# Batches' rising rows turned round in DRAM ahead of their loads, in a fused Fourier and SwiGLU kernel

## The chip, the cores and the metric

The kernel runs on one core of a Trainium2 chip. The metric is device microseconds of one execution; the median of three runs is given. A profiled execution of the same program gives the rows that are quoted below. PE is TensorE, DVE is VectorE, ACT is ScalarE, POOL is GpSimd, SP is SyncE; an SPq row is an instruction with which SP's queue issues a transfer.

## The reference, cut to what matters

```python
def _attn_ref(x):                       # x: 8 batches, 3008 rows, 256 columns
    X = np.fft.fft(x, axis=1)
    X = np.fft.fft(X, axis=2)
    return X.real.astype(np.float32)

def _moe_ref(x, w_gate, w_val, w_out):  # x: 24064 x 256, d_ff 1536
    g = x @ w_gate
    silu = g * (1.0 / (1.0 + np.exp(-g)))
    val = x @ w_val
    return (silu * val @ w_out).astype(np.float32)
```

The output of the first function, its batches laid one after the other, is the input of the second.

## The kernel before, in words

The real part of the transform is even, so the kernel computes rows k and M − k of a batch from the same two halves, an even one (Pt) and an odd one (Qt): plus is their sum, minus their difference. The column transform is multiplied into the weights once (Wp from the cosines, Wq from the sines). The row transform is done per batch: POOL folds the batch's rows into sums and differences ("fold", lines 171 to 205), PE multiplies them with tables (line 1394), and DVE writes Pt and Qt.

**Tiles and units.** The 8 × 1504 columns of Pt and Qt are cut into 24 tiles of at most 512. A unit is one tile with one of twelve blocks of 128 of the 1536 hidden columns: gate and value by four or five matmuls of line 972, SiLU on ACT (1084, 1156, 1159), products for plus on DVE (1186) or POOL (1192), for minus on POOL (1183), which takes the pair buffer sv of two units. The output matmuls with Wo (1236) of one tile run beside the units of the next; ACT evicts them to ev (1243), and SP stores them (1249). A table KINDS gives each unit a digit: bit 0, the value's PSUM bank is filled ahead by ACT (line 1045) and copied out by ACT (1107), otherwise one DVE operation does both (1109); bit 1, the gate is split, with two gate matmuls and two DVE operations (1088, 1152) in place of three matmuls; higher bits, the value is copied by ACT (1189) and the product for plus, or both, go to POOL. The first fourteen units ("w") are done whole.

**Loads of a batch.** Each batch comes as two parts. XA holds 128 groups of rows, XC the other 60 (two batches share it, at partitions 0 and 64). The fold adds rising rows to falling rows, and the kernel wants both in falling order of the partition. "Down sets" are read in that order anyway: four transfers (line 142 for XA, 160 for XC). [...] Batch 0 is loaded once in rising order and turned by PE (line 435). For batch 1 the program writes the mixed order of up and down by hand (C1_ORDER, A1_ORDER); its XC is loaded at both halves of the partitions, by half down sets (line 164) and a copy within SBUF (169). Six of these go out ahead of the units.

**Order.** Behind the beginning, which is written out, a list of operations with engine, length, latency and place is put in order by a small planner (class Sched), which takes on each engine the operation that may start first within a window of places. Shifts (SHIFT) and a table by tile (BIAS_ROWS) move the places. The planner's loads count as SP operations with a time to issue, a landing and a ring time; SP is one queue in order, and each transfer waits for the eighth before it. Weight loads (line 391) and the load of Wo are issued by POOL.

**Steps that the prediction speaks of.** 13.92 us: two clears of XC's unused partitions from a tile of zeros (545). 18.9 us: first unit. 20.9 to 28: weight products for hidden columns 512 to 1535 (1442), whose operands land in XA's memory. 37.7: POOL copies tables (1546). 42.33: fold of batch 1's XC (178), 59.65: of its XA.

Of the kernel before, what the change touches and what calls it, by code (L numbers as in the profile page):

```python
# [12 lines left out]
F32 = mybir.dt.float32  # L13
# [6 lines left out]
def kernel(  # L20
# [8 lines left out]
    nc = tc.nc  # L29
    B, M, D = x.shape  # L30
    Dff = moe_w_gate.shape[1]
    P = 128
# [3 lines left out]
    R = M // 4  # L36
# [16 lines left out]
    NCR = GH - P  # L53
# [52 lines left out]
    XC = const.tile([P, 8, 2, D], F32, name="XC")  # L106
# [24 lines left out]

    JA, JC = P - LA + 1, GH - LC + 1

    C1_EARLY = 6
    C1_ORDER = "uuduuduuduuduumuueuueuece"
    A1_ORDER = "uuuuduuuuduuuuduuuud"

    def load_a(b, q):
        X3 = XA.rearrange("p a q d -> p a (q d)")
        res = ([lambda h=h: q.dma_start(out=X3[LA * h:LA * (h + 1), 0:4, :],  # L140
                                         in_=up_block(b, JA - LA * h, LA)) for h in range(NA)] +
                [lambda a=a: q.dma_start(out=X3[:, 4 + a, :], in_=down_set(b, a, JA, LA, NA)) for a in range(4)])
        return in_order(A1_ORDER, u=res[:NA], d=res[NA:]) if b == 1 else res

    def in_order(order, **todo):
        todo = {k: list(v) for k, v in todo.items()}
        return [todo[k].pop(0) for k in order]

    def load_c(b, q):

        X3 = XC.rearrange("p a q d -> p a (q d)")
        p0 = 64 * (b % 2)
        pm = p0 + NCR
        r = slice(p0, p0 + NCR)
        ups = [lambda h=h: q.dma_start(out=X3[p0 + LC * h:p0 + LC * (h + 1), 0:4, :],
                                       in_=up_block(b, JC - LC * h, LC)) for h in range(NC_)]
        mid = [lambda: q.dma_start(out=XC[pm:pm + 1, 0:4, 1],
                                   in_=rows_at(b, 0, [[R * D, 1], [R * D, 4], [1, D]]))]
        if b != 1:
            return ups + [lambda a=a: q.dma_start(out=X3[r, 4 + a, :], in_=down_set(b, a, JC, LC, NC_))  # L160
                          for a in range(4)] + mid

        def down(a, k):
            q.dma_start(out=XC[0:NCR, 4 + a, 0] if k else XC[r, 4 + a, 0],
                        in_=rows_at(b, R * (a + 1) - 2 * JC + k, [[2 * LC * D, NC_], [-2 * D, LC], [1, D]]))

        downs = [[lambda a=a, k=k: down(a, k) for a in range(4)] for k in range(2)]
        return in_order(C1_ORDER, u=ups, d=downs[0], e=downs[1], m=mid,
                        c=[lambda: q.dma_start(out=XC[0:NCR, 0:4, 1], in_=XC[r, 0:4, 0])])
# [82 lines left out]
    q = nc.sync  # L252
# [104 lines left out]
    sc = 2.0 * math.pi * (1.0 - 2e-7)  # L357
# [28 lines left out]
    def load_w(c, only):  # L386
        for i, src in ((0, moe_w_gate), (1, moe_w_val)):
            if i not in only:
# [13 lines left out]
                        in_=rows_at(0, 0, [[2 * R * D, 2], [R * D, 2], [1, D]]))  # L402
# [141 lines left out]
    for hi in range(2):  # L544
        q.dma_start(out=X3c[64 * hi + NCR:64 * hi + 64, :].rearrange("p (c d) -> p c d", d=D),
                    in_=zeros[64 * hi + NCR:64 * hi + 64].unsqueeze(1).to_broadcast([64 - NCR, 16, D]))
    loads_c1 = load_c(1, q)
    for load in loads_c1[:C1_EARLY]:
        load()
# [142 lines left out]
    A1_LOAD = 8  # L692
    ROW_1 = 12
    ROW_2 = 24
    ROW_3 = 35
    LOAD_AT = 2
# [45 lines left out]
    )  # L742
    BIAS = {(t, k): v for t, row in enumerate(BIAS_ROWS) for k, v in zip(SHIFT, row)}
# [11 lines left out]
    W_AT = (0.0, 2.0, 3.2, 4.6)  # L755
# [164 lines left out]
    def pool_us(n):  # L920
# [9 lines left out]
        "06ww20001013",  # L930
        "031303160011",
        "000010312133",
        "010210112012",
        "10110b103133",
        "001601031052",
        "300171700001",
        "331213005030",
        "010271031001",
        "34130b310300",
        "01b300700101",  # L940
        "21312101b300",
        "001371310011",
        "32120011b212",
        "10130b135030",
        "000135003170",
        "033170001011",
        "213b21011200",
        "103b10319610",
        "4030b13300b0",
        "616404563200",  # L950
        "143034169230",
        "706150233313",
# [21 lines left out]
    S = Sched()  # L974
# [310 lines left out]
    for b in range(2, B, 2):  # L1285
        u = slot[(b, 0)] - 1
# [6 lines left out]
    act_at = {}  # L1293
    spread_at = {}
    loads = []

    def run_loads(n):
        for what, k, fn in loads[:n]:
            up = k < (NA if what[0] == "A" else NC_)
            r, w, us, ring = [], [((what[0],), k)], 0.4 if up else 0.62, 0.57 if up or what[0] == "C" else 1.14  # L1300
            if what == ("A", 1):
                r = [(("C",), C1_ORDER.rindex("u"))]
                us, ring = (0.42, 0.75) if A1_ORDER[k] == "u" else (0.75, 1.1)
            if what == ("C", 1):
                us, ring = (0.48, 0.75) if C1_ORDER[k] == "u" else (0.95, 1.0)
                if C1_ORDER[k] == "c":
                    r = [(("C",), j) for j, o in enumerate(C1_ORDER) if o == "u"]
            S.add("SP", us, fn, r=r, w=w, after=[(("A",), "pre" if A1_ORDER[k] == "d" else "preW")] if what == ("A", 1) else [],
                  lat=2.5, ring=ring)
        del loads[:n]  # L1310
# [4 lines left out]
    def fold_step(what, i, unit):  # L1315
        kind, b = what
        q, j = (1, i) if what == ("C", 1) else divmod(i, 6)
        if i == 0:
            run_loads(max((k + 1 for k, (w_, _, _) in enumerate(loads) if w_ == what), default=0))
# [14 lines left out]
        r = {0: [((kind,), k) for k in range(40)], 1: [(tmp, "F")], 2: [(tmp, "F")], 3: [(tmp, "E"), (tmp, "O")],  # L1334
# [4 lines left out]
        if q == 1 and j == 0:  # L1339
            act_at.setdefault(max(unit + LOAD_AT, 15), []).append(what)  # L1340
# [6 lines left out]
    def load_next(what):  # L1347
        kind, b = what
        if kind == "A":
            if b + 1 < B:  # L1350
                loads.extend((("A", b + 1), k, fn) for k, fn in enumerate(load_a(b + 1, nc.sync)))
        else:
            b = b // 2 * 2 + 2
            if b < B:
                loads.extend((("C", b), k, fn) for k, fn in enumerate(load_c(b, nc.sync) + load_c(b + 1, nc.sync)))
# [248 lines left out]
    for k in range(C1_EARLY):  # L1604
        S.add("DMA", 0.01, lambda: None, w=[(("C",), k)], lat=2.0)
# [3 lines left out]
    S.add("DMA", 0.01, lambda: None, w=[(("pq", 0), "Q")], lat=0.1)  # L1609
# [7 lines left out]
    for i, u in enumerate(units):  # L1617
        t, f = u
# [3 lines left out]
        if i == 1:  # L1622
            loads.extend((("C", 1), k, fn) for k, fn in enumerate(loads_c1) if k >= C1_EARLY)
        if i == A1_LOAD:
            loads[0:0] = ((("A", 1), k, fn) for k, fn in enumerate(load_a(1, nc.sync)))
# [41 lines left out]
    S.run({'DVE': 1.6, 'ACT': 1.0, 'POOL': 1.4, 'PE': 0.0, 'SP': 2.0})  # L1667
# [30 lines left out]
```

## Time and profile before

| | |
|---|---|
| median of 3 runs | 599.71 us (597.59 to 600.29) |
| the profiled execution | 600.4 us |
| its span, first to last instruction | 598.6 us |
| mean granted TensorE clock | 0.999 |
| moved by DMA | 57.65 MB in 51082 packets |

The profiled execution's own time is 1.8 us longer than its span. Busy time counts an engine's instructions once where they overlap; a matmul's end is modelled, so a matmul of 512 columns is shown with 0.37 us though the next one starts 0.2 us after it. Waits are put down to the releaser that came last, and where it is a transfer its name can be that of another on the same semaphore.

### The profile page before, as it was taken

To read this page: it belongs to the slowest core of one execution; us is meant where nothing else is said; L and a number is where in the kernel's file an instruction comes from. 1 tells how busy PE (TensorE), PEld (TensorE's weight loads), DVE (VectorE), ACT (ScalarE), POOL (GpSimd) and SP (SyncE) were. 2 spreads that over 40 slices of the span, in tenths; PEclk is the share of its full clock that TensorE was granted. 3 is DMA by queue.
4 is the path that set the end of the run, shared out by engine and by line. 5 is a ranking of instruction groups with operands and counts; after the bars stand their busy time and mean duration, and the time that the engine had idled before them with its cause. 6 is when DMAs were issued, how large, how long until landed. Compare 5 with 4: busy or idle time off the path is not lost.

```text
span 598.6 us, 12468 instructions
## 1 busy us (share of the span) xinstructions
PE 587.0 (98%) x3953; PEld 389.2 (65%) x4012; DVE 570.3 (95%) x1064; ACT 557.4 (93%) x1080; POOL 527.8 (88%) x486
## 2 busy tenths in 40 slices
PE   7999999999999999999999999999999999999997
PEld 5456666666666666666666666666666666666686
DVE  8989999999999999999999999999999999999993
ACT  8778989989998999999999999999999999999995
POOL 8977999999899999998999998897986868687772
PEclk9999999999999999999999999999999999999999
DMA  9956347454715523454127122046221202111212
GB/s 247 150 110 115 109 121 141 132 140 117 178 46 107 136 70 113 123 129 138 57 55 166 46 62 82 19 115 161 63 64 37 65 19 80 48 46 53 60 54 81
DMA packets 51082, 57.65 MB, mean 96 GB/s; under 512 B 7283, under 2 KB 38439, under 8 KB 51017
## 3 DMA queue, kind: packets, MB, share of 16 engines
q1 hardware_dynamic: 47433, 53.91, 35.2%
q0 software_dynamic: 3216, 2.36, 2.8%
q8 instruction: 31, 0.51, 0.4%
q10 hardware_dynamic: 368, 0.59, 0.3%
q14 instruction: 34, 0.28, 0.2%
HBM read 29.43 MB, written 24.65 MB: 90 GB/s over the span
## 4 chain that ended last, share of the span: by engine, by line
PE 71%; ACT 8%; DMA 6%; DVE 4%; POOL 3%; issue 3%; SPq 1%; ACTq 0%; POOLq 0%; DVEq 0%
PE o L1236 30%; PE g L972 19%; PE v L972 16%; DMA XA<-in_x_dram 5%; ACT sv L1159 2%; PE o L1394 2%; PE g L1394 2%; ACT v L1045 2%; ACT es L1107 1%; POOL hm L1183 1%; DVE sv L1175 1%; ACT sp L1084 1%; DVE hp L1186 1%; ACT sp L1156 1%; ACT ev L1243 1%
## 5 line engine op out<-in xcount | busy, mean ns | idle before, releaser
L1183 POOL TENSOR_TENSOR hm<-sv 128x1024 bf16<-128x1024 f32 (+2 forms) x137 | 254.7, 1862 | 44.1 <-ACT sv L1159 17.7
L1175 DVE SCALAR_TENSOR_TENSOR sv<-es,v 128x512 f32<-128x512 f32 (+2 forms) x262 | 173.6, 668 | 5.4 <-PE v L972 2.8
L1236 PE MATMUL o<-Wo,hm 128*128 128x256 bf16 (+1 forms) x1128 | 163.6, 273 | 0.3
L1236 PE MATMUL o<-Wo,hp 128*128 128x256 bf16 (+1 forms) x1104 | 159.7, 273 | 0.2
L1186 DVE TENSOR_TENSOR hp<-sp,v 128x512 bf16<-128x512 f32 (+2 forms) x233 | 154.2, 668 | 2.8 <-PE v L972 2.0
L1236 PEld LDWEIGHTS <-hm 128*128 128x128 bf16 (+2 forms) x1140 | 111.8, 98 | 57.9 <-issue 2.5
L1236 PEld LDWEIGHTS <-hp 128*128 128x128 bf16 (+2 forms) x1140 | 111.9, 98 | 55.8 <-issue 0.9
L1159 ACT ACTIVATE sv<-g 128x512 f32<-128x512 f32 (+2 forms) x179 | 116.7, 671 | 4.6 <-PE g L972 2.3
L1084 ACT ACTIVATE sp<-g 128x512 f32<-128x512 f32 (+2 forms) x179 | 110.5, 621 | 4.1 <-PE g L972 2.7
L972 PE MATMUL v<-Pt,Wp 128*128 128x512 bf16 (+2 forms) x288 | 105.4, 375 | 1.8 <-DVE hp L1186 0.5
L972 PE MATMUL g<-Pt,Wp 128*128 128x512 bf16 (+2 forms) x280 | 104.4, 374 | 0.9 <-ACT sv L1159 0.7
L1045 ACT ACTIVATE v<-bc,w 128x512 f32<-128x512 bf16 (+2 forms) x146 | 104.6, 717 | 0.4
L1109 DVE SCALAR_TENSOR_TENSOR es<-bc,w,v 128x512 f32<-128x512 bf16 (+2 forms) x128 | 92.6, 731 | 2.4 <-ACT bc L1595 0.8
L1107 ACT ACTIVATE es<-v 128x512 f32<-128x512 f32 (+2 forms) x146 | 90.0, 618 | 3.8 <-PE g L972 1.0
L972 PE MATMUL g<-Qt,Wq 128*128 128x512 bf16 (+2 forms) x247 | 90.5, 374 | 0.4
L972 PEld LDWEIGHTS <-Wp 128*128 128x128 bf16 x576 | 56.3, 98 | 27.8 <-DVE Wp L505 0.7
L972 PE MATMUL g<-Qt,Wm 128*128 128x512 bf16 (+2 forms) x186 | 69.8, 375 | 0.2
L1088 DVE SCALAR_TENSOR_TENSOR sg<-bc,w,g 128x512 f32<-128x512 bf16 (+2 forms) x95 | 68.4, 723 | 1.4 <-PE g L972 0.7
L1159 ACT ACTIVATE sv<-sg 128x512 f32<-128x512 f32 (+2 forms) x95 | 65.1, 692 | 0.2 <-DVE sg L1152 0.2
L1152 DVE SCALAR_TENSOR_TENSOR sg<-sg,g 128x512 f32<-128x512 f32 (+2 forms) x95 | 62.9, 662 | 1.5 <-PE g L972 0.8
L1156 ACT ACTIVATE sp<-g 128x512 f32<-128x512 f32 (+2 forms) x95 | 57.7, 608 | 5.5 <-DVE sg L1152 5.3
L972 PE MATMUL v<-Qt,Wm 128*128 128x512 bf16 (+2 forms) x159 | 59.4, 374 | 0.8 <-ACT es L1107 0.4
(218 smaller groups left out, 759.1 us busy)
## 6 DMA issues: line engine op xcount, KB each, us to landing
out_dram<-ev SPq DMA_DIRECT2D x96, 128.0 KB
XA<-in_x_dram SPq DMA_DIRECT2D x30, 256.0 KB
XA<-in_x_dram SPq DMA_DIRECT2D x112, 64.0 KB
XC<-in_x_dram SPq DMA_DIRECT2D x28, 120.0 KB
XC<-in_x_dram SPq DMA_DIRECT2D x105, 32.0 KB
bc<-br SPq DMA_DIRECT2D x19, 128.0 KB
St<-Fc SPq DMA_DIRECT2D x12, 128.5 KB
out_dram<-ev SPq DMA_DIRECT2D x12, 120.0 KB
```

Of the source, the lines that this page charges most:

```text
L972: nc.tensor.matmul(ps[:, :n], Wt[:, gv, fs], src[:, :n], start=start, stop=stop, skip_group_check=True)
L1045: nc.scalar.activation(T_[kv][:, :w], bc[t][:, :w], AF.Copy, scale=w0[:, 1, f:f + 1])
L1084: nc.scalar.activation(sp_to()[:, :w], T_[kg][:, :w], AF.Silu)
L1088: nc.vector.scalar_tensor_tensor(T_[keg][:, :w], bc[t][:, :w], w0[:, 0, f:f + 1], T_[kg][:, :w], op0=Alu.mult, op1=Alu.add)
L1107: nc.scalar.activation(T_[kes][:, :w], T_[kv][:, :w], AF.Copy, scale=2.0 if on_pool(u) > 1 else 1.0)
L1109: nc.vector.scalar_tensor_tensor(T_[kes][:, :w], bc[t][:, :w], w0[:, 1, f:f + 1], T_[kv][:, :w], op0=Alu.mult, op1=Alu.add)
L1156: nc.scalar.activation(sp_to()[:, :wp], T_[kg][:, :wp], AF.Silu)
L1159: nc.scalar.activation(sv()[:, f % 2, w - 1::-1, 1], T_[kgm if by_dve else kg][:, :w], AF.Silu)
L1175: nc.vector.scalar_tensor_tensor(sv()[:, f % 2, w - 1::-1, 0], T_[kes][:, :w], 2.0, T_[kv][:, :w], op0=Alu.mult, op1=Alu.subtract)
L1183: nc.gpsimd.tensor_tensor(hts_(t)[1][:, f - 1:f + 1, :w], sv()[:, :, :w, 1], sv()[:, :, :w, 0], op=Alu.mult)
L1186: nc.vector.tensor_tensor(hts_(t)[0][:, f, :wp], T_[ksp][:, :wp], T_[kv][:, :wp], op=Alu.mult)
L1236: nc.tensor.matmul(st["ps"][:n, j, :], hts[t][minus][:, f, c:c + n], Wo[:, f, :], start=(f == 0), stop=(f == nF - 1))
```

## The change

Each later batch's rising rows are copied within DRAM to a scratch tile, in falling order of blocks (`reorder`, four copies per part: 256 KB each for XA, 120 KB for XC). XA's rising rows then come in two transfers, XC's in one, whose partitions step forward through the scratch tile. Down sets stay. For batch 1 the copies are issued in the written-out beginning; its XC is filled by eight half down sets and two loads of the turned copy, one for each half of the partitions. For batches 2 and 3 the copies are issued one with each unit from the eleventh on, later ones with every third unit; a load reads all copies that it needs. KINDS, BIAS_ROWS and some due times are new; their numbers are left out below, but for KINDS' counts: of 274 units that aren't whole, split gates go from 95 to 93, values filled ahead from 146 to 139, products for plus on POOL from 41 to 46, with 12 units that give POOL both as before.

```diff
-    C1_EARLY = 6
-    C1_ORDER = "uuduuduuduuduumuueuueuece"
-    A1_ORDER = "uuuuduuuuduuuuduuuud"
+    dram = ctx.enter_context(tc.tile_pool(name="turn", bufs=1, space=bass.MemoryType.DRAM))
+    scratch = {}
+
+    def reorder(kind, b, q):
+        n, L, N, j0 = (P, LA, NA, JA) if kind == "A" else (NCR, LC, NC_, JC)
+        t = scratch[kind, b] = dram.tile([4, N, 2 * L, D], F32, name=f"t{kind}{b}")
+
+        def one(a):
+            q.dma_start(out=t[a].rearrange("h r d -> r h d"),
+                        in_=rows_at(b, R * a + 2 * j0 - 1, [[D, 2 * L], [-2 * L * D, N], [1, D]]))
+
+        return [lambda a=a: one(a) for a in range(4)]
+
+    def reordered(kind, b, a0, a1):
+        return scratch[kind, b][a0:a1].rearrange("a h (i q) d -> (h i) a (q d)", q=2)
 
     def load_a(b, q):
         X3 = XA.rearrange("p a q d -> p a (q d)")
-        res = ([lambda h=h: q.dma_start(out=X3[LA * h:LA * (h + 1), 0:4, :],
-                                         in_=up_block(b, JA - LA * h, LA)) for h in range(NA)] +
+        return ([lambda a=a: q.dma_start(out=X3[:, a:a + 2, :], in_=reordered("A", b, a, a + 2)) for a in (0, 2)] +
                 [lambda a=a: q.dma_start(out=X3[:, 4 + a, :], in_=down_set(b, a, JA, LA, NA)) for a in range(4)])
-        return in_order(A1_ORDER, u=res[:NA], d=res[NA:]) if b == 1 else res
...
     def load_c(b, q):
-
         X3 = XC.rearrange("p a q d -> p a (q d)")
...
+        r = slice(64 * (b % 2), 64 * (b % 2) + NCR)
+        return ([lambda: q.dma_start(out=X3[r, 0:4, :], in_=reordered("C", b, 0, 4))] +
+                [lambda a=a: q.dma_start(out=X3[r, 4 + a, :], in_=down_set(b, a, JC, LC, NC_)) for a in range(4)] +
+                [lambda: mid_c(b, q)])
+
+    def down_c1(a, k, q):
+        q.dma_start(out=XC[slice(0, NCR) if k else slice(64, 64 + NCR), 4 + a, 0],
+                    in_=rows_at(1, R * (a + 1) - 2 * JC + k, [[2 * LC * D, NC_], [-2 * D, LC], [1, D]]))
+
+    def up_c1(k, q):
+        q.dma_start(out=XC[slice(64, 64 + NCR) if k else slice(0, NCR), 0:4, 1],
+                    in_=scratch["C", 1][:].rearrange("a h (i q) d -> q (h i) a d", q=2)[k])
...
-    loads_c1 = load_c(1, q)
-    for load in loads_c1[:C1_EARLY]:
-        load()
+
+    clear_c(1)
+    for k in range(2):
+        for a in range(4):
+            down_c1(a, k, q)
+        if not k:
+            clear_c(0)
+    early = reorder("C", 1, q) + reorder("A", 1, q)
+    for fn in early[:5]:
+        fn()
+    mid_c(1, q)
+    up_c1(1, q)
+    up_c1(0, q)
+    for fn in early[5:]:
+        fn()
     load_w(1, (0,))
...
-    W_AT = (0.0, 2.0, 3.2, 4.6)
+    W_AT = (0.0, 2.3, 3.4, 4.6)
...
         if i == A1_LOAD:
-            loads[0:0] = ((("A", 1), k, fn) for k, fn in enumerate(load_a(1, nc.sync)))
+            loads[0:0] = load_ops("A", 1)
+            pending.extend(reorder_ops("C", 2) + reorder_ops("C", 3) + reorder_ops("A", 2))
+        if i % (1 if i < 26 else 3) == 0 and i > 10:
+            for todo in pending[:1]:
+                del pending[:1]
+                issue(*todo)
+        if i == 26:
+            for b in range(4, B + 2, 2):
+                for ch_, b_ in (("C", b), ("C", b + 1), ("A", b - 1), ("A", b)):
+                    pending.extend(reorder_ops(ch_, b_) if b_ < B else [])
...
-    S.run({'DVE': 1.6, 'ACT': 1.0, 'POOL': 1.4, 'PE': 0.0, 'SP': 2.0})
+    S.run({'DVE': 1.6, 'ACT': 1.0, 'POOL': 1.4, 'PE': 0.0, 'SP': 12.0})
```

The changed program has 489 SP transfers where the one before has 629, and 4008 matmuls where it has 4006. PE's order is the same up to the first transforms of line 1394.

More of the change, by code (lines that the diff above doesn't have):

```diff
@@ L145, in in_order, with mid_c @@
-    def in_order(order, **todo):
-        todo = {k: list(v) for k, v in todo.items()}
-        return [todo[k].pop(0) for k in order]
+    def mid_c(b, q):
+        pm = 64 * (b % 2) + NCR
+        q.dma_start(out=XC[pm:pm + 1, 0:4, 1], in_=rows_at(b, 0, [[R * D, 1], [R * D, 4], [1, D]]))
     def load_c(b, q):
         X3 = XC.rearrange("p a q d -> p a (q d)")
[L152 to L169, printed above, removed]
@@ L692 @@
     A1_LOAD = 8
+    C1_AT_HAND = 17.0
+    A1_TURNED = 18.0
     ROW_1 = 12
@@ L1318, in fold_step @@
         if i == 0:
-            run_loads(max((k + 1 for k, (w_, _, _) in enumerate(loads) if w_ == what), default=0))
+            run_loads(max((k + 1 for k, (w_, _, _) in enumerate(loads) if w_ == what or kind == w_[0] == "C" and w_[1] == b + 1), default=0))
         def fn():
@@ L1603 @@
     S.hold("st", 0)
-    for k in range(C1_EARLY):
-        S.add("DMA", 0.01, lambda: None, w=[(("C",), k)], lat=2.0)
+    S.add("DMA", 0.01, lambda: None, w=[(("C",), 7)], lat=C1_AT_HAND)
+    for k in range(4):
+        S.add("DMA", 0.01, lambda: None, w=[(("sc", "A", 1), k)], lat=A1_TURNED)
     for fc in (1, 2):
```

90 lines of the change are left out of this document (51 added, 39 removed), and 24 rows, old and new, of the table BIAS_ROWS.

## The prediction

> **What bounds the kernel now.** I read the page's busy times first, then busy time by stage, then POOL's timeline and the chain of waits in the one stage where TensorE stands still.
>
> ```profile
> span 598.6 us, 12468 instructions
> PE 587.0 (98%) x3953; PEld 389.2 (65%) x4012; DVE 570.3 (95%) x1064; ACT 557.4 (93%) x1080; POOL 527.8 (88%) x486
> ```
>
> TensorE is busy 98% of the span, so nothing that only shortens another engine or a queue is worth more than the PE idle time it removes. The table by stage says where that idle time lies (stretch, its length, then busy us of each engine, granted clock, DMA share, GB/s).
>
> ```profile
> core 0: us, PE busy (x) PEld busy (x) DVE busy (x) ACT busy (x) POOL busy (x), PEclk, DMA share, GB/s
> 0.00:20.00 20.00, 16.67 (x107) 10.20 (x109) 17.56 (x72) 15.49 (x27) 18.43 (x42) 1.00 0.90 217
> 20.00:40.00 20.00, 19.93 (x119) 9.77 (x120) 17.72 (x34) 16.18 (x34) 17.42 (x30) 1.00 0.74 133
> 40.00:60.00 20.00, 19.84 (x129) 12.90 (x131) 19.21 (x33) 16.34 (x31) 14.81 (x16) 1.00 0.67 116
> 60.00:110.00 50.00, 48.16 (x326) 31.81 (x327) 46.98 (x88) 44.37 (x86) 49.76 (x47) 1.00 0.53 130
> 110.00:200.00 90.00, 89.41 (x605) 60.06 (x615) 87.87 (x159) 84.84 (x165) 86.15 (x80) 1.00 0.50 123
> 200.00:300.00 100.00, 99.47 (x667) 65.64 (x675) 98.25 (x178) 96.49 (x185) 97.42 (x84) 1.00 0.38 103
> 300.00:400.00 100.00, 99.32 (x666) 65.86 (x676) 98.01 (x175) 97.51 (x188) 95.42 (x83) 1.00 0.30 75
> 400.00:500.00 100.00, 99.33 (x667) 65.67 (x677) 97.45 (x179) 96.88 (x187) 79.81 (x66) 1.00 0.27 71
> 500.00:580.00 80.00, 79.63 (x552) 54.36 (x557) 77.87 (x134) 77.96 (x157) 62.74 (x42) 1.00 0.19 55
> ```
>
> Length minus PE busy is 0.07 and 0.16 us in the two stages from 20 to 60, **1.84 us from 60 to 110**, and 0.59, 0.53, 0.68, 0.67 and 0.37 us after it, 2.84 together. So from 20 to 580 all that a better order can win is 0.07 + 0.16 + 1.84 + 2.84 = 4.91 us. In the stage that loses most, POOL is busy 49.76 of 50 us, while in the stage before it POOL idled 20 − 14.81 = 5.19 us. POOL's timeline shows what it idled for (start, duration, instruction, idle time before it and who ended it).
>
> ```profile
> 37.72 2.55 POOL L1546 COPY Tab<-Tab 64x752 bf16<-64x752 bf16 x3
> 42.33 2.36 POOL L178 TENSOR_TENSOR SDf<-XC 128x1020 f32<-128x1020 f32 x1 [2.06 <-DMA XA<-in_x_dram]
> ...
> 55.72 1.89 POOL L1183 TENSOR_TENSOR hm<-sv 128x1024 bf16<-128x1024 f32 x1 [0.72 <-DVE sv L1175]
> 59.65 2.36 POOL L178 TENSOR_TENSOR SDf<-XA 128x1020 f32<-128x1020 f32 x1 [2.03 <-DMA out_dram<-ev]
> ```
>
> Both waits of 2 us stand before the first fold step of a batch: batch 1's rows in XC (42.33) and in XA (59.65). The releaser names in brackets come from a queue that many transfers share; the instruction is the fold, and what it reads is XC and XA. The chain of waits confirms it and shows who pays.
>
> ```profile
> 52.45 6.81 DMA XA<-in_x_dram
> ...
> 81.13 1.86 POOL hm L1183
> 83.01 0.65 ACT sv L1159
> 83.71 0.59 PE g L972 x2
> ```
>
> The last down set of batch 1 is issued at 52.45 and lands 6.81 us later, at 59.26. POOL then works without a break until its product hm at 81.13; ACT may refill the pair buffer sv only after that, and PE waits for ACT. So late rows cost POOL 4 us, and POOL's backlog costs PE up to 1.84.
>
> **The change, part by part.** *Loads of batch 1.* SP's order after the change, from 13.92 on: one clearing store, four half down sets, a clear, four half down sets, four C copies and one A copy in DRAM, the middle row, two loads of XC from the turned copy (which wait for the four C copies), three A copies, one C2 copy, four down sets of XA, two loads of XA. SP's own rows give the price of an issue.
>
> ```profile
> 13.92 1.50 SPq L545 DMA_DIRECT2D XC<-Z  x2
> 15.46 3.69 SPq L155 DMA_DIRECT2D XC<-in_x_dram  x2
> 19.19 0.92 SPq L164 DMA_DIRECT2D XC<-in_x_dram  x1
> 20.16 1.03 SPq L155 DMA_DIRECT2D XC<-in_x_dram  x2
> ...
> 42.59 0.58 SPq L142 DMA_DIRECT2D XA<-in_x_dram  x1
> ```
>
> Clears and half sets take 2 × 0.75 + 8 × 0.92 = 8.9 us, to 22.8. No row shows a copy from DRAM to DRAM; its issue is bounded by 0.58 (a 256 KB set) and 0.92, and I take 0.75, between these two: five copies end at 26.5. A landing is bounded below by nothing but the issue and above by the chain's 6.81; I take 5, nearer to that row since transfers are queued there. XC's copies are then in DRAM at about 31, the two loads issued by 33, XC complete at about 38; with 6.81 twice it is about 42, as now. Three A copies, a C2 copy and four down sets end at 33 + 4 × 0.75 + 4 × 0.58 = 38.3. The last A copy is issued at about 35.3 and lands at about 40; the two loads of XA go out by 41.5 and land by 47 to 49. SP also stood once: the pair at 15.46 took 3.69 us where the pair at 20.16 took 1.03. The same standstill would shift all of this by 2.7 us, XC to 41 and XA to 50 to 52, and 2 us more in each of three landings XA to 58, still before 59.26. So the wait of 2.03 us before XA goes, and perhaps the 0.72. XC is less sure: POOL's new order puts its first fold step ahead of three of the four table copies of L1546 (2.55 us), so POOL asks for XC at 37.7. At 38 POOL wins 2.06 − 0.3 = 1.8 us; at 41 it stands 3.3 us and loses 3.3 − 2.06 = 1.2 against now. POOL is ahead of its present place by 2.03 + 0.72 + 1.8 = 4.5 us at best and by 2.03 − 1.2 = 0.8 at worst when it comes to the stretch from 60 to 110. Of PE's 1.84 us there I take **−1.3** (bounds −1.84 and 0), nearer to the full gain since the late landings are the less likely ones. What is late next is POOL itself, whose work from 60 to 110 stays.
>
> *Loads of batches 2 to 7.* SP issues 140 DMAs fewer (489 against 629), and the copies add 7 × (1024 + 480) KB, 10.5 MB beside the 57.65 MB moved now. PE's and POOL's rows after 110 show next to no wait for loads (POOL's whole idle time from 200 to 300 is 2.6 us, at a DMA share of 0.38), so the fewer issues win nothing there and the extra bytes have room: **0**.
>
> *The weights.* The copies share the DMA engines with the last three weight loads, which GpSimd issues.
>
> ```profile
> 18.00:23.00 5.00, 4.76 (x24) 2.06 (x24) 4.62 (x14) 2.98 (x7) 4.34 (x11) 1.00 1.06 168
> 23.00:28.00 5.00, 4.93 (x24) 2.20 (x24) 5.00 (x10) 4.29 (x10) 4.25 (x7) 1.00 0.85 138
> ...
> XA<-in_moe_w_gate_dram POOLq DMA_DIRECT2D x2, 256.0 KB, 6.3
> XA<-in_moe_w_val_dram POOLq DMA_DIRECT2D x2, 256.0 KB, 8.6
> ...
> L1442 PEld LDWEIGHTS <-CD 128*128 128x128 bf16 x8 | 0.7, 97 | 1.1 <-DMA XA<-in_moe_w_gate_dram 0.5 <-DMA XA<-in_moe_w_val_dram 0.2
> ```
>
> PE already waits 0.5 and 0.2 us for them, so the load path has no slack, and PE's order is unchanged there. By 23 us SP now issues 480 KB of half sets, where it issued two clears, six 32 KB blocks and two half sets or so: some 0.2 MB more, 1.2 us at 168 GB/s if all of it went ahead of the weights. Transfers interleave and the first copies start only after the half sets; I take **+0.3** (bounds 0 and 1.2).
>
> *The units.* KINDS has two units fewer with a split gate, seven fewer with a value seeded ahead, and five more whose product goes to POOL.
>
> ```profile
> 23.40 0.59 PE L1442 MATMUL o<-XA,CD 128*128 128x512 bf16 x2
> 23.83 0.59 PE L1442 MATMUL o<-XA,SDt 128*128 128x512 bf16 x2
> ...
> L1186 DVE TENSOR_TENSOR hp<-sp,v 128x512 bf16<-128x512 f32 (+2 forms) x233 | 154.2, 668 | 2.8 <-PE v L972 2.0
> L1045 ACT ACTIVATE v<-bc,w 128x512 f32<-128x512 bf16 (+2 forms) x146 | 104.6, 717 | 0.4
> L1109 DVE SCALAR_TENSOR_TENSOR es<-bc,w,v 128x512 f32<-128x512 bf16 (+2 forms) x128 | 92.6, 731 | 2.4 <-ACT bc L1595 0.8
> L1107 ACT ACTIVATE es<-v 128x512 f32<-128x512 f32 (+2 forms) x146 | 90.0, 618 | 3.8 <-PE g L972 1.0
> ...
> L1192 POOL TENSOR_TENSOR hp<-sp,pp 128x512 bf16<-128x512 f32 (+1 forms) x41 | 51.2, 1251 | 4.4 <-ACT pp L1189 2.3 <-ACT sp L1156 1.9
> L1189 ACT COPY pp<-v 128x512 f32<-128x512 f32 (+1 forms) x41 | 24.9, 608 | 3.6 <-DVE sv L1175 3.1 <-PE v L972 0.3
> ```
>
> Each unit that isn't split has a third gate matmul; two matmuls of 512 columns start 23.83 − 23.40 = 0.43 us apart from the next pair: **+0.43**, on the bound engine and not to be hidden. ACT loses 7 × (0.717 + 0.618) = 9.3 and gains 5 × 0.608 = 3.0 us; DVE gains 7 × 0.731 = 5.1 and loses 5 × 0.668 = 3.3, less the gate work of two splits; POOL gains 5 × 1.251 = 6.3 us, against the 20.19 and 17.26 it idles after 400. None of it is PE time, so its worth is the PE idle it makes or unmakes, between −2.84 (all of it after 110) and about +3 (as much again); that idle is 0.6% of its stage already, so I take **0**, where each stage's row stands.
>
> Before 14 us and in the tail after 580 the order of work stays. **Sum:** −1.3 + 0.3 + 0.43 = −0.6 us, from the profiled execution's own 600.4 (span 598.6 and 1.8 around it) to 599.8. That execution lies 0.7 above the median of the runs, 599.71, so I forecast 599.71 − 0.6 = **599.1 us**. A measurement of this kernel tells about 0.5% from no change, 3.0 us: under 596.7 is faster, over 602.7 slower.
>
> **Rivals.**
> 1. *The new order empties PE's other gaps too.* For it: POOL may get 4.5 us back and ACT 6.3. Against: after 110 PE idles in crumbs, and DVE is at 97 to 98%. With all 4.91 us gone and 0.73 added it is 599.71 − 4.2 = 595.5; with most, about **596.0**.
> 2. *Slower: the copies hold the weights back.* Place: 23 to 28 us, the loads of columns 512 to 1535. Until the last weight lands, SP may put 0.48 MB of C copies and 0.25 MB of A on the same engines; 0.73 MB at 138 to 168 GB/s is 4.3 to 5.3 us. PE waits for these loads already, so a later landing is passed on to it; from 3.9 us of delay on (−1.3 + 0.43 + 3.9 = 3.0) it decides, and at 4.8, the middle, it gives 599.71 − 0.9 + 4.8 = **603.6**. For it: DMA share 1.06 and PE's 0.5 us wait. Against: SP's issues of 0.75 to 0.92 us space the copies out, and they come after most of the weights' time. The Trainium skill ("DMA: Bandwidth & Descriptors", section "Issuing engines are not separate DMA queues") says that DMAs started by different engines run on the same 16 DMA engines and interleave; by that rule the copies do slow GpSimd's weight loads, and the trace agrees as far as its share passes 1 where both overlap.
> 3. *The new units fit worse.* Planned due times that the chip doesn't keep leave DVE or ACT late, at 97% and over 96% busy from 200 on; PE's 2.84 us after 110 doubled, and 1 us on top, is +3.8 on the forecast: **602.9**.
> 4. *The change doesn't do what it says.* A copy needs two landings where a load needs one; if each takes over 8 us, XA is as late as now and XC later, POOL waits as now, and 599.71 + 0.73 = **600.4** is left.
>
> **How the numbers follow.** Forecast 0.45 (599.1), rival 4 0.09 (600.4): within 0.5% together 0.54. Rival 1 0.21 (596.0): faster. Rivals 2 and 3 0.13 and 0.12 (603.6, 602.9): slower, 0.25. The range reaches from rival 1 with most gaps gone, 595.8, to rival 2, 603.6, and leaves out the far ends of both; the forecast's own range, from its bounds for POOL (−1.84 to 0) and the weights (0 to 1.2), is 598.3 to 601.3.
>
> **What would show it.** POOL's first SDf<-XA near 55 to 58 instead of 59.65 with no wait for a DMA before it, SDf<-XC at 38 to 41, and PE busy over 49.5 us of 60 to 110 make the gain right. PE's waits at the weight products, 0.5 and 0.2 now, grown by a few tenths make the cost right; grown by 2 us or more, rival 2. PE idle from 110 to 580 near 2.8 us makes the nothing for the units right; 5 us or more, rival 3. A POOL wait for XC or XA as long as now is rival 4. The forecast is wrong as a whole if store or load waits on SP hold ACT's evictions back, of which the trace of before shows no sign.

## The result, and the profile after

| | before | after |
|---|---|---|
| median | 599.79 us (597.59 to 601.94, 20 runs) | 598.36 us (597.96 to 598.75, 20 runs) |
| the profiled execution | 600.4 us, span 598.6 | 598.26 us, span 596.5 |

The ratio is 0.9976 (interval 0.9969 to 0.9983): 1.43 us faster, under the 0.5% that stood for "no change". Before's executions spread over 4.35 us, after's over 0.79. The profiled executions lie 2.1 us apart, more than the medians, since that of before is one of its longer ones. Four executions in a slower state, one of 1044 us in e3, one of 2216 in g1, one of 1829 of before beside f1 and f1's own longest, enter no ratio, and the ranges of e3 and g1 leave theirs out.

The page of after: span, busy time, bytes moved, SP's DMA queue (packets, MB, share of 16 engines' span) and the engines' shares of the chain that ended last.

```profile
span 596.5 us, 12394 instructions
PE 589.7 (99%) x4014; PEld 389.9 (65%) x4014; DVE 568.3 (95%) x1062; ACT 553.7 (93%) x1071; POOL 533.4 (89%) x491
...
DMA packets 61294, 68.17 MB, mean 114 GB/s; under 512 B 6968, under 2 KB 48892, under 8 KB 61230
...
q1 hardware_dynamic: 57646, 64.44, 37.2%
...
PE 96%; DVE 0%; ACT 0%; issue 0%
```

Before's page has, for the last two:

```profile
q1 hardware_dynamic: 47433, 53.91, 35.2%
...
PE 71%; ACT 8%; DMA 6%; DVE 4%; POOL 3%; issue 3%; SPq 1%; ACTq 0%; POOLq 0%; DVEq 0%
```

The chain of after hardly leaves TensorE: DMA's 6%, ACT's 8% and POOL's 3% are gone from it. That goes with the order of the engines more than with the loads: below, f2 has after's order and batch 1's old loads and 94% on PE, g1 has before's order and batch 1's new loads and 79%. The copies' 10.5 MB are there and cost SP's queue 2 points of share. After's busy time by stage (columns as in the prediction's table):

```profile
20.00:40.00 20.00, 19.93 (x120) 9.93 (x121) 17.80 (x36) 16.48 (x34) 15.67 (x28) 1.00 0.88 179
40.00:60.00 20.00, 20.00 (x132) 12.93 (x131) 19.10 (x33) 15.74 (x30) 19.42 (x20) 1.00 0.82 259
60.00:110.00 50.00, 50.00 (x347) 33.71 (x346) 49.09 (x93) 46.08 (x91) 49.69 (x48) 1.00 0.54 157
110.00:200.00 90.00, 90.00 (x611) 59.50 (x610) 85.94 (x159) 85.65 (x166) 88.01 (x81) 1.00 0.50 149
200.00:300.00 100.00, 100.00 (x679) 65.92 (x678) 97.62 (x172) 94.44 (x181) 95.96 (x81) 1.00 0.47 133
```

PE's 1.84 us of idle time from 60 to 110 are gone. POOL is busy 19.42 us from 40 to 60 where it was busy 14.81, and by 60 us it has done 18.18 + 15.67 + 19.42 = 53.3 us of work (18.18 from 0 to 20) where it had done 18.43 + 17.42 + 14.81 = 50.7.

**A trap in this table.** That PE also idles 0.00 us after 110, where before showed 2.84, is mostly not a gain. Before's trace has 3953 matmul records to 4012 weight loads, after's 4014 to 4014. An experiment below, e5, runs after's very order on the four engines, and its trace lacks records again:

```profile
200.00:300.00 100.00, 99.48 (x668) 65.86 (x677) 97.56 (x172) 94.39 (x181) 95.90 (x81) 1.00 0.38 99
```

It takes the same time, 598.29 us, and shows 0.52 us of "idle" for 11 matmuls fewer than after's 679: 0.05 us for each record that is missing. So below I don't use the idle column. I use **stalls**, worked out from the trace by matmul: the time from one start to the next, less the pitch at which undisturbed ones follow each other (0.216 us for 512 columns, 0.109 for 256), with missing records counted at that pitch from the program's order. Each row of the tables below is one profiled execution; the two of before differ by up to 0.5 us in a stage.

| us of stall | 19 to 40 | 40 to 60 | 60 to 100 | 100 to 150 | 150 to 580 | sum |
|---|---|---|---|---|---|---|
| before | 1.51 | 0.06 | 1.96 | 0.64 | 1.88 | 6.05 |
| before, profiled again | 1.65 | 0.35 | 1.68 | 0.16 | 2.12 | 5.96 |
| after | 1.36 | 0.00 | 0.08 | 0.25 | 1.34 | 3.03 |

3.0 us fewer, less 0.43 for two more matmuls and 0.27 for a first unit that starts at 19.13 instead of 18.86, makes 2.3; PE's last matmul ends 2.38 us earlier.

POOL's timeline of after shows its folds of batch 1 (start, duration, instruction, idle time before it):

```profile
39.81 2.35 POOL L181 TENSOR_TENSOR SDf<-XC 128x1020 f32<-128x1020 f32 x1 [2.02 <-DMA tA<-in_x_dram]
42.13 0.20 POOL L182 TENSOR_TENSOR EOf<-XC 128x4 f32<-128x4 f32 x1
42.27 0.81 POOL L1605 COPY Tab<-Tab 64x752 bf16<-64x752 bf16 x1
...
54.97 2.36 POOL L181 TENSOR_TENSOR SDf<-XA 128x1020 f32<-128x1020 f32 x1 [0.22 <-DMA tA<-in_x_dram]
```

XA's fold starts 4.7 us earlier and waits 0.22 us instead of 2.03. XC's still waits 2.02 us, but 2.5 us sooner and with the table copies behind it. Not all of the 4.7 us is the loads': f2 below, with after's order and batch 1 in blocks, folds XA at 56.71, 2.9 us earlier than before. SP's timeline of after gives the loads:

```profile
15.18 4.47 SPq L167 DMA_DIRECT2D XC<-in_x_dram  x4
19.69 0.72 SPq L548 DMA_DIRECT2D XC<-Z  x1
20.46 3.53 SPq L167 DMA_DIRECT2D XC<-in_x_dram  x4
24.03 4.10 SPq L142 DMA_DIRECT2D tC<-in_x_dram  x4
28.17 0.59 SPq L142 DMA_DIRECT2D tA<-in_x_dram  x1
28.81 0.68 SPq L157 DMA_DIRECT2D XC<-in_x_dram  x1
35.13 0.85 SPq L171 DMA_DIRECT2D XC<-tC  x2
36.02 1.89 SPq L142 DMA_DIRECT2D tA<-in_x_dram  x3
...
42.30 1.03 SPq L152 DMA_DIRECT2D XA<-tA  x2
```

and SP's waits of after from 12 to 62 us (us in total, times, longest):

```profile
SPq L171 <- DMA tC<-in_x_dram: 5.5, 2, 3.6
...
SPq L142 <- DMA XC<-Z: 1.1, 1, 1.1
...
SPq L142 <- DMA XC<-in_x_dram: 0.3, 1, 0.3
```

The four C copies stand in a row of 4.10 us, but 1.4 us of it are SP's waits for earlier transfers (the last two lines); by the trace, the issue of one took 0.63 to 0.69 us. The last is out at 28.13, and the first load of the turned copy goes out at 35.13, 7.0 us later; SP stands 5.5 us of that, with A's last three copies behind it.

### The profile page after: what moved, and what is told of

Read it like the earlier page. It is cut to its first block, busy times and chain, and to the rows that moved or that the text cites. A ratio compares the mean times of both kernels' runs of the same rounds, so it can differ in the third digit from the quotient of the medians.

```text
span 596.5 us, 12394 instructions
## 1 busy us (share of the span) xinstructions
PE 589.7 (99%) x4014; PEld 389.9 (65%) x4014; DVE 568.3 (95%) x1062; ACT 553.7 (93%) x1071; POOL 533.4 (89%) x491
## 3 DMA queue, kind: packets, MB, share of 16 engines
q1 hardware_dynamic: 57646, 64.44, 37.2%
## 4 chain that ended last, share of the span: by engine, by line
PE 96%; DVE 0%; ACT 0%; issue 0%
PE o L1279 41%; PE g L1015 27%; PE v L1015 21%; PE g L1453 2%; PE o L1453 2%; PE v L1279 1%; PE o L1501 1%; PE g L622 0%; PE o L622 0%; PE g L1279 0%; PE o L1582 0%; PE g L1650 0%; DVE Wp L508 0%; ACT es L1289 0%
## 5 line engine op out<-in xcount | busy, mean ns | idle before, releaser
L1229 DVE TENSOR_TENSOR hp<-sp,v 128x512 bf16<-128x512 f32 (+2 forms) x228 | 151.5, 671 | 1.9 <-PE v L1015 1.1
L1127 ACT ACTIVATE sp<-g 128x512 f32<-128x512 f32 (+2 forms) x181 | 112.0, 620 | 5.8 <-PE g L1015 4.3
L1015 PE MATMUL g<-Pt,Wp 128*128 128x512 bf16 (+2 forms) x288 | 107.5, 374 | 0.0
L1015 PE MATMUL g<-Qt,Wq 128*128 128x512 bf16 (+2 forms) x288 | 105.4, 375 | 0.0
L1088 ACT ACTIVATE v<-bc,w 128x512 f32<-128x512 bf16 (+2 forms) x139 | 100.3, 725 | 1.9 <-DVE sv L1218 0.9
L1152 DVE SCALAR_TENSOR_TENSOR es<-bc,w,v 128x512 f32<-128x512 bf16 (+2 forms) x135 | 97.8, 732 | 2.1
L1150 ACT ACTIVATE es<-v 128x512 f32<-128x512 f32 (+2 forms) x139 | 86.1, 622 | 3.2 <-PE v L1015 1.6
L1015 PE MATMUL g<-Qt,Wm 128*128 128x512 bf16 (+2 forms) x195 | 73.1, 376 | 0.0
L1235 POOL TENSOR_TENSOR hp<-sp,pp 128x512 bf16<-128x512 f32 (+1 forms) x46 | 57.2, 1247 | 8.0 <-ACT pp L1232 7.8
L1015 PEld LDWEIGHTS <-Wq 128*128 128x128 bf16 x437 | 42.7, 98 | 27.5 <-issue 0.4
```

The costliest lines, as they stand in the source:

```text
L1015: nc.tensor.matmul(ps[:, :n], Wt[:, gv, fs], src[:, :n], start=start, stop=stop, skip_group_check=True)
L1088: nc.scalar.activation(T_[kv][:, :w], bc[t][:, :w], AF.Copy, scale=w0[:, 1, f:f + 1])
L1127: nc.scalar.activation(sp_to()[:, :w], T_[kg][:, :w], AF.Silu)
L1150: nc.scalar.activation(T_[kes][:, :w], T_[kv][:, :w], AF.Copy, scale=2.0 if on_pool(u) > 1 else 1.0)
L1152: nc.vector.scalar_tensor_tensor(T_[kes][:, :w], bc[t][:, :w], w0[:, 1, f:f + 1], T_[kv][:, :w], op0=Alu.mult, op1=Alu.add)
L1229: nc.vector.tensor_tensor(hts_(t)[0][:, f, :wp], T_[ksp][:, :wp], T_[kv][:, :wp], op=Alu.mult)
```

## The experiments

Two theories stood against each other. **The loads' theory (theory 1):** batch 1's rows arrive sooner, POOL comes to 60 us less late, and PE's stalls from 60 to 100 go; the new units only fit themselves to it. **The units' theory (theory 2):** the gain is the newly searched KINDS and BIAS_ROWS, and the loads are hidden anyway. A third question was what the copies themselves cost. Ratios are to the kernel before on the same chip. "Blocks" are the loads of rising rows of the kernel before: sixteen transfers of 8 partitions for XA, fifteen of 4 for XC.

### e1_old_units: after, with the KINDS and BIAS_ROWS of before

```diff
-    KINDS, BIAS_ROWS as in after
+    KINDS, BIAS_ROWS as in before
```

> All turned loads of the change, with KINDS and BIAS_ROWS of the kernel before (so two matmuls fewer than the changed kernel). Theory 1 (batch 1's rows come sooner, POOL is ahead from 60 to 110 us): the gain stays and 0.43 us of PE work isn't paid, about 597.9 to 598.8, PE idle from 60 to 110 near nothing. Theory 2 (the units searched anew make the gain, the loads nothing): about 599.8, PE's stalls of 0.5 to 0.9 us from 60 to 110 still there.

Measured: 609.69 us (609.28 to 610.15), ratio 1.017 (1.0156 to 1.0184).

### e2_new_units: before, with the KINDS and BIAS_ROWS of after

```diff
-    KINDS, BIAS_ROWS as in before
+    KINDS, BIAS_ROWS as in after
```

> All loads as before, with KINDS and BIAS_ROWS of the changed kernel. Theory 1: no gain, and the 0.43 us of two more matmuls on top, 600.2 or more, POOL waiting about 2 us for XC near 40 and for XA near 58. Theory 2: the whole gain, about 598.4.

Measured: 614.62 us (614.25 to 617.04), ratio 1.026 (1.0241 to 1.028).

### e3_first_only: after, with batch 1 turned and batches 2 to 7 loaded by blocks

```diff
     def load_a(b, q):
+        if b != 1:
+            return ([lambda h=h: q.dma_start(out=X3[LA * h:LA * (h + 1), 0:4, :],
+                                             in_=up_block(b, JA - LA * h, LA)) for h in range(NA)] + ...
...
-            pending.extend(reorder_ops("C", 2) + reorder_ops("C", 3) + reorder_ops("A", 2))
```

> Only batch 1 is turned in DRAM; batches 2 to 7 load in blocks as before; units as in the changed kernel. Theory 1: as the changed kernel, 598.0 to 598.8. Theory 3 (the later batches' fewer, wider transfers make the gain): back to about 599.8 or more, with POOL or PE waits behind loads after 110 us.

Measured: 615.98 us (613.39 to 616.66), ratio 1.0266 (1.0245 to 1.0286).

### e4_later_only: after, with batch 1 loaded as before

```diff
+    def old_a(b, q): ...
+    def old_c(b, q): ...
-    loads_c1 = load_c(1, q)
+    loads_c1 = old_c(1, q)
```

> Batch 1 loads as before (blocks, half sets, copy within SBUF); batches 2 to 7 are turned in DRAM; units as in the changed kernel. Theory 1: no gain, 599.8 to 600.5, POOL's fold of batch 1's XA near 59 again. Theory 3: about 598.4.

Measured: 603.37 us (602.94 to 605.04), ratio 1.0069 (1.0054 to 1.0084).

**What follows from these four.** Every mixture is slower than both kernels, and neither theory gives that. The loads are entries of the planner's list; with other entries it puts the work of all engines in another order, and the units and shifts were searched for the order that they came with. The stall table shows it:

| us of stall | 19 to 40 | 40 to 60 | 60 to 100 | 100 to 150 | 150 to 580 | sum |
|---|---|---|---|---|---|---|
| e1_old_units | 1.42 | 0.06 | 0.16 | 0.26 | 12.94 | 14.84 |
| e2_new_units | 2.44 | 0.00 | 0.91 | 0.59 | 14.77 | 18.71 |
| e3_first_only | 1.52 | 0.00 | 0.14 | 0.25 | 17.23 | 19.14 |
| e4_later_only | 1.36 | 0.00 | 1.70 | 0.43 | 4.65 | 8.14 |

Up to 100 us the loads' theory holds: with batch 1 turned the stalls from 60 to 100 are 0.16 (e1) and 0.14 (e3), with its blocks 1.70 (e4) and 0.91 (e2). What sets the time comes after 150. In e1's table by stage, 300 to 400 is the worst stretch:

```profile
300.00:400.00 100.00, 94.93 (x615) 60.09 (x623) 92.06 (x162) 91.01 (x173) 87.40 (x77) 1.00 0.22 63
```

5.07 us of PE idle at a DMA share of 0.22, with DVE, ACT and POOL idle beside it: engines waiting for each other, not for loads. e1's waits name no transfer from 110 to 580 us. So the units' worth can't be had by swapping tables; the next kernels keep the order of PE, DVE, ACT and POOL of one of the two kernels to the instruction, and change only what SP's entries do.

### f1_later_blocks: after's order; batches 2 to 7 by blocks, without their copies

Each wide load's place issues its eight or fifteen blocks in one bunch.

```diff
+        def blocks(k):
+            for h in range(NA // 2 * k, NA // 2 * (k + 1)):
+                q.dma_start(out=X3[LA * h:LA * (h + 1), 0:4, :], in_=up_block(b, JA - LA * h, LA))
+        if b > 1:
+            return ([lambda k=k: blocks(k) for k in range(2)] + ...
-        return [lambda a=a: one(a) for a in range(4)]
+        return [lambda a=a: one(a) if b == 1 else None for a in range(4)]
```

> The changed kernel's order on TensorE, VectorE, ScalarE and GpSimd, instruction for instruction; only SP differs: batches 2 to 7 load in blocks of 8 and 4 partitions, issued where the one or two wide loads stood, and their copies in DRAM are left out. If the 12 to 17 us of the runs that mixed loads and units came from the planner's other order, this stays at 598.0 to 599. If they came from late block loads on the chip, 605 or more, with POOL waiting for XA or XC after 110 us.

Measured: 628.12 us (619.77 to 633.22), ratio 1.0432 (1.038 to 1.0485). f1's waits (us in total, times, longest), the second line SP's own, before it issues a store:

```profile
ACT ev L1300 <- DMA out_dram<-ev: 12.1, 5, 5.1
...
SPq L1306 <- DMA XA<-in_x_dram: 12.9, 26, 0.8
```

A bunch keeps the stores behind it from going out (in SP's timeline one of fifteen blocks takes 6.00 us, and the next three stores follow it), and ACT waits up to 5.1 us for an eviction buffer; neither before nor after has any wait of ACT for a transfer, and before spreads its blocks over many units. In f1's trace the granted TensorE clock also falls to 0.5 in four stretches of 3.4 us, at 82, 198, 256 and 345 us, where after's stays at 1.0: up to 6.8 of its 24.35 us of stall are slower matmuls. f1 shows what a bunch on SP costs, not what before's spread-out blocks cost: after's order with those was not tried, and that share of the change stays open.

### f2_first_blocks: after's order; batch 1 loaded by blocks as before

```diff
-    early = reorder("C", 1, q) + reorder("A", 1, q)
-    ...
+    for load in old_c(1, q):
+        load()
```

> Again the changed kernel's order on the four engines; only batch 1 loads as before (blocks, half sets, copy within SBUF). Theory 1 (batch 1's rows come sooner): POOL waits for XC and XA, PE's stalls from 40 to 110 come back, 600 to 602. Theory 4 (the order is what counts, not the loads): 598.4 to 599.

Measured: 600.40 us (598.81 to 603.91), ratio 1.003 (1.0011 to 1.005). XC's loads have before's mix; XA's sixteen blocks go out in two bunches behind its down sets, not in before's mix. POOL's timeline of f2:

```profile
41.48 2.35 POOL L216 TENSOR_TENSOR SDf<-XC 128x1020 f32<-128x1020 f32 x1 [2.98 <-DMA XC<-in_x_dram]
...
56.71 2.36 POOL L216 TENSOR_TENSOR SDf<-XA 128x1020 f32<-128x1020 f32 x1 [0.30 <-DMA tC<-in_x_dram]
```

XA's fold stands 2.9 us ahead of before's 59.65 and 1.7 behind after's 54.97: most of after's lead at XA comes from the new order, the rest from the loads.

### e5_no_copies: after's order; no copies, rising rows straight from the input

The rising rows come in as wide as in after but not turned round, so other rows meet in the fold.

```diff
-        return [lambda a=a: one(a) for a in range(4)]
+        return [lambda: None] * 4
...
-        return scratch[kind, b][a0:a1].rearrange("a h (i q) d -> (h i) a (q d)", q=2)
+        return rows_at(b, R * a0 + 1, [[2 * D, n], [R * D, a1 - a0], [1, 2 * D]])
```

> The changed kernel's order on the four engines without any copy in DRAM: rising rows are loaded straight from the input, not turned round (so they stand in the wrong partitions). If the copies' traffic is free, 598.2 to 598.6; if it costs PE the few tenths that were forecast for the weights, 597.9 or less, with the first unit or the weight products sooner.

Measured: 598.31 us (598.20 to 599.40), ratio 0.9987 (0.9977 to 0.9998). After's ratio is 0.9976 (0.9969 to 0.9983): the copies and their landings cost nothing that can be measured. Against f2, measured beside it in the same order, e5 is 2.1 us faster, and the intervals of the two ratios don't touch. f2 still makes the copies of batches 2 to 7, but after makes them too and is no slower than e5; so in after's order the 2.1 us are what batch 1's loads by blocks cost. f2's table by stage and its weight products of columns 512 to 1535 (count | busy us, mean ns | idle before, releasers) show both places:

```profile
20.00:40.00 20.00, 19.41 (x115) 9.31 (x117) 16.93 (x34) 15.93 (x34) 15.26 (x27) 1.00 0.69 124
...
60.00:110.00 50.00, 49.17 (x337) 33.09 (x339) 48.53 (x91) 45.50 (x89) 49.76 (x47) 1.00 0.66 184
```

```profile
L1523 PEld LDWEIGHTS <-CD 128*128 128x128 bf16 x8 | 0.6, 98 | 1.8 <-DMA XA<-in_moe_w_gate_dram 0.8 <-DMA XA<-in_moe_w_val_dram 0.6
```

The weight loads for PE wait 1.4 us there. In after the same row names no DMA:

```profile
L1501 PEld LDWEIGHTS <-CD 128*128 128x128 bf16 x8 | 0.8, 97 | 1.0 <-issue 0.2
```

### f3_first_unturned: before's order; batch 1's rising rows in one transfer each, not turned

No copies; in batch 1's fold other rows meet.

```diff
+        if b == 1:
+            one = lambda: q.dma_start(out=X3[:, 0:4, :], in_=up_block(1, 1, P))
+            return in_order(A1_ORDER, u=[one] + [lambda: None] * (NA - 1), d=res[NA:])
...
+        ups = [lambda: q.dma_start(out=X3[r, 0:4, :], in_=up_block(1, 1, NCR))] + [lambda: None] * (NC_ - 1)
```

> The order of the kernel before on the four engines; batch 1's rising rows come in one transfer for XA and one for XC, straight from the input and so not turned round (its rising rows stand in the wrong partitions). Theory 1: POOL's waits of 2 us go and PE's 1.5 to 2 us of stalls from 60 to 110 with them, 597.7 to 598.5. Theory 4: 599.7, as before.

Measured: 600.70 us (599.38 to 603.07), ratio 1.0024 (1.0012 to 1.0036). POOL's folds find their rows at 41.14 and 58.47 without a wait, and the stalls from 60 to 100 are gone (0.15), yet its median is higher. In its trace the last weights land at 28.5 us, where before has 27.3 and, profiled again, 27.9, and the weight loads wait 1.8 us for them. That execution, 599.38 us, is f3's fastest and shorter than before's profiled one, so what makes the median higher isn't shown.

```profile
L1447 PEld LDWEIGHTS <-CD 128*128 128x128 bf16 x8 | 0.6, 97 | 2.1 <-DMA XA<-in_moe_w_gate_dram 0.9 <-DMA XA<-in_moe_w_val_dram 0.9
```

### g1_first_turned_old_order: before's order and units; batch 1 loaded as in after

Batches 2 to 7 keep their blocks.

```diff
-    loads_c1 = load_c(1, q)
-    for load in loads_c1[:C1_EARLY]:
-        load()
+    clear_c(1)
+    ...                                   # after's beginning: half sets, copies, up_c1
+    loads_c1 = [lambda: None] * len(C1_ORDER)
...
+            return in_order(A1_ORDER, u=[wide] + [lambda: None] * (NA - 1), d=res[NA:])
```

> The order of the kernel before on the four engines, with its units; batch 1 is turned in DRAM and loaded as in the changed kernel, batches 2 to 7 load in blocks as before. Theory 1 with theory 5 (batch 1's old C loads also hold the weights back, more in some executions than in others, which spreads the times over 4 us): the whole gain without the two more matmuls, 597.3 to 598.0, fastest to slowest within 1.3 us, PE's stalls from 60 to 100 gone. If the new units or the later loads carry part of the gain: 598.4 or more.

Measured: 598.76 us (598.31 to 599.17), ratio 0.999 (0.9979 to 1.0001). POOL's timeline and the table by stage of g1:

```profile
40.47 2.34 POOL L211 TENSOR_TENSOR SDf<-XC 128x1020 f32<-128x1020 f32 x1
...
55.93 1.89 POOL L1229 TENSOR_TENSOR hm<-sv 128x1024 bf16<-128x1024 f32 x1 [2.05 <-DVE sv L1221]
57.78 2.36 POOL L211 TENSOR_TENSOR SDf<-XA 128x1020 f32<-128x1020 f32 x1
```

```profile
60.00:110.00 50.00, 49.84 (x344) 33.60 (x345) 48.87 (x92) 46.39 (x90) 49.76 (x49) 1.00 0.51 130
```

Both folds run without a wait, 1.9 us sooner than before, and PE loses nothing but missing records from 60 to 110. POOL's 2 us before XA's fold have not gone, though: in this order POOL now waits as long for DVE's sv, one product earlier. The spread falls to 0.86 us, like after's, as expected. The median falls by 0.35 only, into the branch in which the units or the later loads carry part of the gain.

### g2_xa_unturned: before's order; only XA's rising rows in one transfer, not turned

In the fold of batch 1's XA other rows meet; XC is loaded as before.

```diff
+        if b == 1:
+            one = lambda: q.dma_start(out=X3[:, 0:4, :], in_=up_block(1, 1, P))
+            return in_order(A1_ORDER, u=[one] + [lambda: None] * (NA - 1), d=res[NA:])
```

> The order of the kernel before; XC of batch 1 as before; its XA rising rows in one transfer straight from the input, not turned round (so they stand in the wrong partitions). Theory 1: the 2 us wait before the fold of XA goes and PE's stalls from 60 to 100 shrink from 1.9 to under 1 us. Theory 5: the spread of 3 to 4 us stays, the median is 598.6 to 599.7. Without theory 5: 598.3 or less and a narrow spread.

Measured: 599.56 us (598.93 to 600.72), ratio 1.0007 (0.9995 to 1.0019). XA's fold no longer waits, but in this profile the weights landed at 28.5 us, though nothing that SP issues before then differs from before:

```profile
L1445 PEld LDWEIGHTS <-CD 128*128 128x128 bf16 x8 | 0.6, 97 | 2.3 <-DMA XA<-in_moe_w_gate_dram 1.2 <-DMA XA<-in_moe_w_val_dram 0.7
```

So the 0.7 us that before's profile shows there varies from one execution to the next.

### g4_xc_only: before's order; only batch 1's XC as in after

```diff
-    loads_c1 = load_c(1, q)
+    early = reorder("C", 1, q)
+    ...                                   # after's beginning without the A copies
```

> The order of the kernel before; XC of batch 1 turned in DRAM as in the changed kernel, XA in blocks as before. Theory 5: the last weights land by 26 us and the spread shrinks to 1.3 us. Theory 1: XA is still folded near 58, PE's stalls from 60 to 100 stay over 1 us; 598.3 to 599.3. Without theory 5: the spread stays at 3 to 4 us.

Measured: 599.09 us (598.27 to 599.91), ratio 0.9998 (0.9988 to 1.0009). Only the median came as expected: the last weights land at 27.1 us, the times spread over 1.64 us, and XA is folded at 58.38 with stalls of 0.16 from 60 to 100. Before itself, profiled once more beside these (g3_before_again):

> The kernel before once more, for a second profile of it. Theory 1: POOL waits 2 us for XC and XA and PE stalls near 2 us from 60 to 100 again. Theory 5: its last weight load lands at another time than 27.3 us, and the time differs from 600.4 by about as much as the weight products do.

It took 600.40 us, with the stalls that stand in the second row of the first stall table.

| us of stall | 19 to 40 | 40 to 60 | 60 to 100 | 100 to 150 | 150 to 580 | sum |
|---|---|---|---|---|---|---|
| f1_later_blocks | 1.49 | 0.00 | 4.03 | 2.56 | 16.27 | 24.35 |
| f2_first_blocks | 2.18 | 0.00 | 0.88 | 0.29 | 1.29 | 4.64 |
| e5_no_copies | 1.44 | 0.00 | 0.08 | 0.25 | 1.42 | 3.19 |
| f3_first_unturned | 2.31 | 0.05 | 0.15 | 0.26 | 1.83 | 4.60 |
| g1_first_turned_old_order | 1.47 | 0.06 | 0.16 | 0.30 | 2.05 | 4.04 |
| g2_xa_unturned | 2.61 | 0.05 | 0.15 | 0.28 | 2.07 | 5.16 |
| g4_xc_only | 1.49 | 0.06 | 0.16 | 0.30 | 2.03 | 4.04 |

**What follows.** In before's order, batch 1's rows in time are enough for the stalls from 60 to 100: g1 has both parts in time, and in g4 XA's blocks are no longer late either, since SP comes to them sooner. g2 mends XA alone with the same result, but there PE comes 1.1 us later by its longer stall from 19 to 40, which may help. So the loads' theory is shown for that stage, with one limit: the new order alone, with batch 1 in blocks, has 0.88 there (f2), half of before's.

For the whole time the answer hangs on the order. In after's order undoing batch 1's loads costs 2.1 us (f2 against e5), more than the whole gain; in before's order they win 0.35 us of the 1.43 (g1, whose interval reaches to nothing and overlaps after's). What after's trace has beyond g1's is 0.7 us less stall from 150 to 580, in an order made for the wider loads, minus 0.43 for two matmuls. Nor do the profiled stalls pass one for one into the medians of before's order: g1's profiled execution is 1.5 us shorter than before's, its median 0.35. Both profiled executions of before, 600.4, lie over a us above the median beside g1, 599.11; what its other executions wait for isn't shown.

## Why the prediction was right, by its steps

- **Batch 1's loads, −1.3 us for PE from 60 to 110: right for the stage, and somewhat larger; not shown as a saving of the loads alone.** From 60 to 100 the stalls fall by 1.9 us (1.6 against the second profile of before). The loads alone take off 1.8 in before's order (g1) and 0.8 in after's (f2 to after); in medians they are worth 0.35 us in the one and 2.1 in the other. XA's fold came at 54.97 (forecast 55 to 58) with next to no wait, XC's at 39.81 (38 to 41). A copy's issue took less than the 0.75 us that were taken (0.63 to 0.69 for C, 0.59 for A), but SP stood 1.4 us among the four, and their landing was mis-sized: 7.0 us after the last issue where 5 was taken. XC's wait did not shrink; POOL is 2.6 us ahead at 60, between the 0.8 and 4.5 worked out.
- **Later loads, 0: held for the copies.** e5 leaves out all of them and is no faster. What the wide loads of batches 2 to 7 gain over spread-out blocks is not told apart from the new order; together with the units the two leave 0.5 to 0.8 us less stall from 150 to 580.
- **The weights, +0.3: wrong in sign.** The last weight load lands at 25.8 us instead of 27.3 (27.9 in the second profile), and the 0.7 us that the weight loads waited for transfers at these products went; PE's stalls from 19 to 40 fell by 0.15 us (0.29 against the second profile). The copies have no part in it: without them (e5) it lands at 25.7. It goes with the beginning of XC's loads: the seven profiles with that of after have the last weights between 25.1 and 27.1 us, the seven with that of before, f3's among them, between 27.3 and 28.5. PE's stalls from 19 to 40 us are 1.36 to 1.52 in the former and 1.36 to 2.61 in the latter. The step counted the bytes that SP issues by 23 us, and these went up; whether the blocks, the order of half sets and rising rows, or the copy within SBUF keep the weights longer was not told apart (f3, with one wide transfer in the place of XC's blocks, is as late as any). The Trainium skill ("DMA: Bandwidth & Descriptors", section "Issuing engines are not separate DMA queues") says that transfers started by different engines interleave on the same DMA engines; that the landing of GpSimd's loads goes with the order of SP's agrees with it. **Rival 2 fell**: its 3.9 us of delay would have come from the copies.
- **The units, +0.43 and 0 beyond that: held for this combination alone, and the 0 by luck.** The two matmuls are paid, and stalls after 110 didn't double: **rival 3 fell**. e1 and e2 show what each kernel's tables cost with the other's loads, 10 and 15 us; the zero came out, but the step had no reason for it, since it left out that the planner's order hangs on the loads' entries. **Rival 1** (596.0) named what is left over in part: the gaps after 100 shrank, but from about 2.4 to 1.6 us and not from 2.84 to nothing, since most of the idle time that it counted was missing records. **Rival 4 fell** with XA's wait. By the sign that was set for it, a wait for XC or XA as long as now, XC's 2.02 us would have spoken for it; the sign was badly chosen, since POOL now asks for XC sooner.
- **The sum.** −1.3 + 0.3 + 0.43 = −0.6 stands against −1.43, both inside the 0.5%, and the forecast's range holds no change too; so the steps say more than the number. The weights' term of +0.3 turned out below nothing, and the crumbs after 100 gave 0.7 to 0.9 where 0 was taken. That after's executions spread over 0.79 us instead of 4.35 was not forecast. It goes with batch 1's loads, in either order: 0.86 with them turned in before's (g1), 5.1 with them undone in after's (f2). That the weights' landing makes the spread isn't shown: in g2 they land as late as in any run, and it spreads over 1.79 us.

No kernel here beats after; e5 only equals it.

## What to carry to other kernels

When an order is planned, a load's length is part of the plan: change loads and tuned tables together, and judge one change by holding the order of all engines still and altering only what the DMA entries do. Before reading tenths of idle time in a table by stage, compare the matmul records with the weight loads; 11 missing records in 100 us looked like half a microsecond of gain. A wait removed in one stage is worth what the medians say, not what one profiled execution shows.

## What the runs showed of the hardware

In these profiled executions, turning rows round within DRAM was nearly free in queue time, and loading them wide paid for part of it. e5's page, with the wide loads and no copies, has

```profile
q1 hardware_dynamic: 46446, 53.66, 32.0%
```

so the same 53.7 to 53.9 MB take 32.0% of the 16 engines' span in wide loads (in e5 not turned) and 35.2% (34.1% in the second profile) with blocks of 4 and 8 partitions. The copies' 64.44 − 53.66 = 10.8 MB add 5.2 points, and what remains on balance is 2 to 3 points for a fifth more bytes. What they ask for is time to land, 7.0 us here; of a price in throughput the times show nothing.
